# Down products of a gated MLP two blocks behind its gates, and the last down products of the MLP before it in one group

## The chip, the cores and the metric

The kernel runs on one core of a Trainium2 chip. The metric is the device time of one launch in microseconds. Before the change it is 898.23 us, the median of 3 runs (897.46 to 899.17).

## What is computed

Windowed attention (4 batches, 8 heads, 576 positions, head width 64), then a first MLP that takes the maximum of three products, then a gated MLP, on 2304 tokens of width 512, all in fp32:

```python
def _attn_ref(q, k, v):              # window 128, bias by head
    scores = np.where(mask, scale * q @ k.T + bias, -1e9)
    return softmax(scores) @ v
def _moe_ref(x, w1, w2, w3, w_out):  # 512 -> 768 -> 512
    h = np.maximum(np.maximum(x @ w1, x @ w2), x @ w3)
    return h @ w_out
def _moe2_ref(x, w_gate, w_val, w_out):  # 512 -> 1536 -> 512
    g = x @ w_gate
    silu = g * (1.0 / (1.0 + np.exp(-g)))
    return (silu * (x @ w_val)) @ w_out
```

## The kernel before

**Arithmetic.** TensorE multiplies in fp32r. Every fp32 operand is split into a head (rounded to fp32r) and a rest (value minus head), and a product of two operands is three matmuls: head by head, head by rest, rest by head. `mm3` (L111 to L113) does this for the up products of the first MLP and the gate and value products of the second; L547 to L549 do it for the down products of the second.

**Splitting the weights.** `prep_w` turns a raw weight piece of 128x512 into head and rest: one activation on ScalarE (L90, into `wf`), three operations on VectorE (L93, L94, L96), the cast of the head on ScalarE (L99), and the rest on VectorE (`low`, L77). It is done for 18 up pieces `w` of the first MLP (`prep_up`), its down pieces `wo`, and 36 pieces `u` of the second MLP (`prep`: gate, value and down piece of each of 12 blocks of the hidden width).

**Splitting the activations.** GpSimd rounds heads with `pool_round` (L80) and takes rests with `low` (L77): `x` from the attention, `h` from the first MLP, `a` from the gated product. In `gate`, ScalarE takes the sigmoid (L532), VectorE multiplies twice (L533, L534) into `sg`, and GpSimd makes head and rest of `a`.

**The stages.** The tokens of a batch fall into two sub-blocks of 256 and 320 tokens; there are eight, in the list `order`. For each the attention runs in steps (scores, normalise, transpose, values `pv`), `up_groups` gives 18 groups of 12 matmuls, and `down_groups` four rows of output in three groups, 72 matmuls in all. `spread` writes the groups of one list with the steps of others in between, so that attention steps and weight preparation stand among the products. The second MLP goes through five chunks of up to 512 tokens; a block (c, f) is 24 gate and value matmuls and 12 down matmuls for one twelfth of the hidden width. Before, `gate` of the next block stands ahead of the `down` of this one. `load_y` fetches the first MLP's output, which `down_groups` stores to `y_dram`; `YAT` is the block at which the next chunk's is loaded.

**What sets the order.** A scheduler orders each engine's instructions from the written order and priorities: `high_priority` pulls a piece forward; `keep_in_program_order`, used in `prep_w` where `pinned` is true, holds the first activation (L90) in its written place. Each engine then works through its own list in order.

**Buffers that matter here.** PSUM: four tiles of the pool `ps_m`, shared by the up and down groups and the gates; one tile `pv` for the attention's values; four tiles `ps_o` for the second MLP's output. The values of a unit leave `pv` by one ScalarE copy (L394) and three VectorE additions (L395, and L397 twice) into `xr`, and GpSimd splits `xr` into `x`.

Of the kernel before, what the change touches and what calls it, by code (L numbers as in the profile page):

```python
# [23 lines left out]
NF1, NF2 = F1 // P, F2 // P  # L24
# [5 lines left out]
CHUNKS = [(t, min(TB, NT - t)) for t in range(0, NT, TB)]  # L30
FILL = -float(2.0 ** 100)

RAWS = 4
C0, C1, C2, C3 = 5, 6, 12, 15
HIGH, EARLY = 100, 3
NORM = "aa"
A2, A3 = 4, 2
D6 = 0
WARM, WN = 24, 256
NORM0, K0 = "pp", 4  # L40
AH = 0, 100
A1, E1 = 3, 0
YAT = 8
LN, LT, LV = 1, 2, 4

LEAST = 1.0 * 2.0 ** -15
PIN = False


@with_exitstack  # L50
def kernel(ctx: ExitStack, tc, q0, k0, q1, k1, qk0, qk1, vv, w123, wo1, wgv, wo2, out):
# [87 lines left out]
    def up_groups(b, s):  # L139

        n = SUBS[s][1]
        m = {}

        def group(f, e):
            xt = x_t[b, s]
            ps = ps_m.tile([P, 512], F32, tag="m", name="ps1")
            for k in range(KD):
                mm3(ps[:, :n], w1[f, e], k * P, xt[k][:, 0, :n], xt[k][:, 1, :n], k == 0, k == KD - 1)
            with tc.high_priority(HIGH):
                if e == 0:  # L150
                    m[f] = tmp.tile([P, 320], F32, tag="m0", name="m0")
                    nc.scalar.copy(m[f][:, :n], ps[:, :n])
                else:
                    nc.vector.tensor_tensor(out=m[f][:, :n], in0=ps[:, :n], in1=m[f][:, :n], op=ALU.max)
                if e == 2:
                    ht = hp.tile([P, 2, n], F32R, tag=f"h{s}", name=f"h{s}", bufs=NF1)
                    pool_round(ht[:, 0, :], m[f][:, :n])
                    low(nc.gpsimd, ht[:, 1, :], m[f][:, :n], ht[:, 0, :])
                    hs[b, s, f] = ht

        return [lambda f=f, e=e: group(f, e) for f in range(NF1) for e in range(3)]

    def down_groups(b, s):
        t0, n = SUBS[s]
        t0 += b * S

        def part(ps, d, ks):
            for k in ks:
                ht = hs[b, s, k]
                mm3(ps[:, :n], wo[k], d * P, ht[:, 0, :], ht[:, 1, :], k == 0, k == NF1 - 1)  # L170

        def group(ds):

            ps = [ps_m.tile([P, 512], F32, tag="m", name="ps2") for d in ds]
            for i, d in enumerate(ds):
                part(ps[i], d, range(NF1 - 1))
            for i, d in enumerate(ds):
                part(ps[i], d, [NF1 - 1])
                with tc.high_priority(HIGH):
                    y = tmp.tile([P, 2, 320], F32R, tag="y", name="y")  # L180
                    nc.scalar.copy(y[:, 0, :n], ps[i][:, :n])
                    low(nc.vector, y[:, 1, :n], ps[i][:, :n], y[:, 0, :n])
                nc.sync.dma_start(
                    out=y_dram[:, d * P:(d + 1) * P, t0:t0 + n].rearrange("a p n -> p a n"),
                    in_=y[:, :, :n].bitcast(F32),
                )

        return [lambda ds=ds: group(ds) for ds in ((0, 1), (2,), (3,))]

    order = [(b, s) for b in range(B) for s in range(2)]  # L190
# [4 lines left out]
    prep = ea("prep", 4)  # L195
# [253 lines left out]
    for t in range(len(units) + LV):  # L449
# [9 lines left out]
        if t < len(units):  # L459
            u = units[t]  # L460
            if u.j == BLOCKS[u.s][0]:
                i = todo.index((u.b, u.s, u.p))
# [6 lines left out]
    def attn_units(i):  # L469
        return steps[done_at[i]:done_at[i + 1]]  # L470

    def spread(main, *others, early=0):


        done = [0] * len(others)
        for i, g in enumerate(main):
            for n, o in enumerate(others):
                while done[n] < len(o) and done[n] * (len(main) - early) <= i * len(o):
                    o[done[n]]()
                    done[n] += 1  # L480
            g()
        for n, o in enumerate(others):
            for piece in o[done[n]:]:
                piece()
# [90 lines left out]
    conv = [lambda f=f, e=e: prep_up(f, e) for f in range(NF1) for e in range(3)]  # L575
# [9 lines left out]
    spread(up_groups(*order[2]), a3[len(a3) * A3 // 8:], early=EARLY)  # L585
    for i in range(3, len(order) - 1):
        spread(down_groups(*order[i - 1]) + up_groups(*order[i]), attn_units(i + 1), early=EARLY)
    for g in down_groups(*order[-2])[:D6]:
        g()
    actx.close()  # L590
    raws2 = en("raws2", RAWS)
    w2pool = en("w2pool")
    ps_o = en("ps_o", 4, space=PSUM)
    prep, load_y, gate, down = second(w2pool, raws2, ps_o)
    conv = [lambda f=f, i=i: prep(f, i) for f in range(NF2) for i in range(3)]
    spread(down_groups(*order[-2])[D6:] + up_groups(*order[-1]), [lambda: load_y(0, [0])] + conv[:C2])
    spread(down_groups(*order[-1]), [lambda: load_y(0, [1])] + conv[C2:C3])

    spread([lambda: gate(0, 0)], conv[C3:C3 + 3])
    blocks = [(c, f) for c in range(len(CHUNKS)) for f in range(NF2)]
    for n, (c, f) in enumerate(blocks):
        if c == 0:
            for piece in conv[C3 + 3 + 3 * f:C3 + 6 + 3 * f]:
                piece()
        if f == YAT and c + 1 < len(CHUNKS):
            load_y(c + 1)
        if n + 1 < len(blocks):
            gate(*blocks[n + 1])  # L610
        for t in range(CHUNKS[c][1] // P):
            down(c, t, f)

# [55 lines left out]
```

## Time and profile before

| what | value |
|---|---|
| median of 3 runs | 898.23 us (897.46 to 899.17) |
| profiled execution | 900.01 us |
| its span | 898.3 us |
| mean granted clock of TensorE | 0.996 |
| TensorE matmul (PE) busy | 878.1 us, 98% |
| VectorE (DVE) busy | 464.6 us, 52% |
| GpSimd (POOL) busy | 409.3 us, 46% |
| ScalarE (ACT) busy | 349.5 us, 39% |

The profiled execution is a single one; its own time contains its span and 1.7 us around it. The shares are averages over the whole span. The attention and the first MLP take about the first half, and the other engines are busy mostly there: in the page's forty slices VectorE is at 0.6 to 0.9 up to the twenty-third and at 0.1 in nearly all of the rest. A stretch must therefore be read by itself. Granted clock 1.00 is 2.4 GHz for TensorE, 0.50 is 1.2 GHz. The end of a matmul in the trace is modelled, so that one row overlaps the next; the distance of two starts is the better measure of its cost.

### The profile page before, as it was taken

How to read it: one execution, taken by the hardware profiler on the slowest of the kernel's cores; microseconds unless marked ns; L12 is line 12 of the kernel's file. 1: busy time of each engine (PE TensorE's matmuls, PEld its weight loads, DVE VectorE, ACT ScalarE, POOL GpSimd, SP SyncE). 2: the span in 40 equal slices, each digit the busy share in tenths (PEclk: the TensorE clock that was granted, in tenths of full speed). 3: DMA queues.
4: the chain of work that ended last, by engine and by line, in shares of the span. 5: the costliest groups of instructions: out<-in, count | busy, mean ns of one | idle time of the engine just before them, and what ended most of it. 6: DMA issues, size and time to landing. Idle time of an engine off the chain costs nothing.

```text
span 898.3 us, 14855 instructions
## 1 busy us (share of the span) xinstructions
PE 878.1 (98%) x5280; PEld 778.7 (87%) x5280; DVE 464.6 (52%) x1293; ACT 349.5 (39%) x1004; POOL 409.3 (46%) x599
## 2 busy tenths in 40 slices
PE   8998999999999999999998999999999999999998
PEld 6677899999999999999886788888888888888897
DVE  7689956867687776848999811111111111111111
ACT  6789656856486656614554301000110001000101
POOL 5587666766777586554325421222122212221222
PEclk9899999999999999999999999999999999999999
DMA  9844414415232431325755504000210002000100
GB/s 324 281 122 128 135 45 153 126 55 148 67 113 60 137 99 51 116 93 170 257 184 176 165 0 141 1 1 1 93 48 1 1 21 73 1 1 1 47 1 24
DMA packets 40873, 82.22 MB, mean 92 GB/s; under 512 B 3680, under 2 KB 16992, under 8 KB 40800
## 3 DMA queue, kind: packets, MB, share of 16 engines
q1 hardware_dynamic: 39712, 79.18, 27.5%
q10 hardware_dynamic: 1088, 2.10, 0.7%
q8 instruction: 42, 0.69, 0.3%
q14 instruction: 31, 0.25, 0.1%
HBM read 67.11 MB, written 14.16 MB: 90 GB/s over the span
## 4 chain that ended last, share of the span: by engine, by line
PE 81%; issue 6%; POOL 5%; DVE 4%; DMA 1%; ACT 1%; ACTq 0%; SPq 0%; POOLq 0%; DVEq 0%
PE ps L111 10%; PE pg L111 10%; PE pg L112 10%; PE pg L113 10%; PE ps L113 10%; PE ps L112 10%; PE po L549 5%; PE po L547 5%; PE po L548 5%; PE pv L390 2%; PE pt L349 2%; POOL a L80 1%; PE sc L299 1%; PE sc L304 1%; PE sc L303 1%
## 5 line engine op out<-in xcount | busy, mean ns | idle before, releaser
L80 POOL TENSOR_SCALAR a<-sg 128x512 fp32r<-128x512 f32 (+1 forms) x60 | 44.5, 742 | 331.8 <-DVE sg L534 328.5
L113 PE MATMUL pg<-y,u 128*128 128x512 f32 (+1 forms) x480 | 176.6, 368 | 0.0
L112 PE MATMUL pg<-y,u 128*128 128x512 f32 (+1 forms) x480 | 176.5, 368 | 0.0
L111 PE MATMUL pg<-y,u 128*128 128x512 f32 (+1 forms) x480 | 176.5, 368 | 0.0
L113 PE MATMUL ps<-x,w 128*128 128x256 f32 (+1 forms) x576 | 173.5, 302 | 1.6 <-DVE w L77 1.5
L111 PE MATMUL ps<-x,w 128*128 128x256 f32 (+1 forms) x576 | 173.3, 304 | 1.2 <-ACT w L99 1.2
L112 PE MATMUL ps<-x,w 128*128 128x256 f32 (+1 forms) x576 | 172.3, 300 | 1.9 <-POOL x L77 1.9
L533 DVE TENSOR_TENSOR sg<-pg,sg 128x512 f32<-128x512 f32 (+1 forms) x60 | 38.2, 637 | 253.8 <-ACT sg L532 253.8
L532 ACT ACTIVATE sg<-pg 128x512 f32<-128x512 f32 (+1 forms) x60 | 33.2, 553 | 325.2 <-PE pg L113 321.8
L113 PEld LDWEIGHTS ps<-x,w 128*128 128x128 f32 x576 | 109.2, 190 | 4.2 <-DVE w L77 2.4
L111 PEld LDWEIGHTS ps<-x,w 128*128 128x128 f32 x576 | 109.0, 190 | 4.0 <-ACT w L99 1.5
L112 PEld LDWEIGHTS ps<-x,w 128*128 128x128 f32 x576 | 109.2, 190 | 2.7 <-POOL x L77 2.1
L111 PEld LDWEIGHTS pg<-y,u 128*128 128x128 f32 x480 | 90.5, 188 | 15.5
L112 PEld LDWEIGHTS pg<-y,u 128*128 128x128 f32 x480 | 90.5, 188 | 15.3
L113 PEld LDWEIGHTS pg<-y,u 128*128 128x128 f32 x480 | 90.5, 188 | 15.1
L365 POOL TENSOR_SCALAR_AFFINE_SELECT t<-pk 128x512 fp32r<-128x512 f32 (+3 forms) x128 | 72.7, 590 | 34.7 <-PE pv L390 14.5
L549 PE MATMUL po<-u,a 128*128 128x512 f32 x216 | 84.2, 392 | 2.8 <-POOL a L77 2.8
L547 PE MATMUL po<-u,a 128*128 128x512 f32 x216 | 84.4, 391 | 0.3 <-POOL a L80 0.3
L548 PE MATMUL po<-u,a 128*128 128x512 f32 x216 | 84.2, 390 | 0.0
L77 POOL TENSOR_TENSOR a<-sg,a 128x512 fp32r<-128x512 f32 (+1 forms) x60 | 72.4, 1206 | 5.0
L317 ACT ACTIVATE z<-z,mn 128x128 f32<-128x128 f32 (+1 forms) x160 | 63.3, 399 | 21.8 <-DVE mn L312 21.8
L534 DVE TENSOR_TENSOR sg<-pg,sg 128x512 f32<-128x512 f32 (+1 forms) x60 | 38.2, 637 | 60.3 <-PE pg L113 60.1
(91 smaller groups left out, 1672.4 us busy)
## 6 DMA issues: line engine op xcount, KB each, us to landing
wr<-wgv SPq DMA_DIRECT2D x24, 512.0 KB, 4.2
qkr<-qk SPq DMA_DIRECT2D x24, 416.0 KB, 3.4
wr<-w SPq DMA_DIRECT2D x18, 512.0 KB, 5.2
wr<-wo SPq DMA_DIRECT2D x12, 512.0 KB, 3.9
y<-y_dram SPq DMA_DIRECT2D x12, 512.0 KB, 4.1
y_dram<-y SPq DMA_DIRECT2D x16, 320.0 KB, 2.4
out<-ob SPq DMA_DIRECT2D x18, 256.0 KB, 2.1
y_dram<-y SPq DMA_DIRECT2D x16, 256.0 KB, 2.9
```

Source lines behind the costliest of these rows:

```text
L77: eng.tensor_tensor(out=out, in0=raw, in1=head.bitcast(F32), op=ALU.subtract)
L80: nc.gpsimd.tensor_scalar(out=out, in0=in_, scalar1=1.0, scalar2=1.0, op0=ALU.mult, op1=ALU.mult)
L111: nc.tensor.matmul(ps, wh, xt_h, start=first, stop=False)
L112: nc.tensor.matmul(ps, wh, xt_l, start=False, stop=False)
L113: nc.tensor.matmul(ps, wl, xt_h, start=False, stop=last)
L317: nc.scalar.activation(out=z[:m, a], in_=z[:m, a], func=AF.Exp, scale=-1.0, bias=mn[:m, a:a + 1], accum_out=sm[:m, a:a + 1],)
L365: nc.gpsimd.affine_select(out=t[:, i, :n, :, :m], in_=w[:, :n, :, :m], compare_op=op, fill=0.0, base=0, pattern=[[0, n], [0, 2], [-sign, m ...
L533: nc.vector.tensor_tensor(out=sg, in0=pair[0], in1=sg, op=ALU.mult)
L534: nc.vector.tensor_tensor(out=sg, in0=pair[1], in1=sg, op=ALU.mult)
L547: nc.tensor.matmul(po, ah, w2[f, 2][:, 0, :], start=f == 0, stop=False)
L548: nc.tensor.matmul(po, ah, w2[f, 2][:, 1, :], start=False, stop=False)
L549: nc.tensor.matmul(po, al, w2[f, 2][:, 0, :], start=False, stop=f == NF2 - 1)
```

## The change

It changes five things.

1. In the second MLP, the gates of two blocks stand ahead of the first `down`, and inside the loop `gate` runs two blocks ahead instead of one.
2. The pieces `u` are prepared in the order in which this needs them: gate and value pieces of two blocks, then for each block f the gate and value pieces of f + 2 and the down piece of f.
3. The down products of the last sub-block but one are no longer ahead of the last up products: they come behind them, in one list with the down products of the last sub-block. 18 pieces instead of 15 are written ahead of the first gates.
4. `PIN`: the first activation of each up piece keeps its written place on ScalarE. `C0`: four instead of five up pieces are prepared beside the first attention steps.
5. `YAT`: the next chunk's input is loaded at block 6 instead of 8.

```diff
-C0, C1, C2, C3 = 5, 6, 12, 15
+C0, C1, C2, C3 = 4, 6, 12, 18
...
-D6 = 0
...
-YAT = 8
+YAT = 6
...
-PIN = False
+PIN = True
...
-    for g in down_groups(*order[-2])[:D6]:
-        g()
...
-    conv = [lambda f=f, i=i: prep(f, i) for f in range(NF2) for i in range(3)]
-    spread(down_groups(*order[-2])[D6:] + up_groups(*order[-1]), [lambda: load_y(0, [0])] + conv[:C2])
-    spread(down_groups(*order[-1]), [lambda: load_y(0, [1])] + conv[C2:C3])
-    spread([lambda: gate(0, 0)], conv[C3:C3 + 3])
     blocks = [(c, f) for c in range(len(CHUNKS)) for f in range(NF2)]
+    need = [(f, i) for f in range(2) for i in range(2)]
+    for f in range(NF2):
+        need += [(f + 2, i) for i in range(2) if f + 2 < NF2] + [(f, 2)]
+    conv = [lambda f=f, i=i: prep(f, i) for f, i in need]
+    spread(up_groups(*order[-1]), [lambda: load_y(0, [0])] + conv[:C2])
+    spread(down_groups(*order[-2]) + down_groups(*order[-1]), [lambda: load_y(0, [1])] + conv[C2:C3])
+    spread([lambda: gate(0, 0), lambda: gate(0, 1)], conv[C3:C3 + 3])
     for n, (c, f) in enumerate(blocks):
...
-        if n + 1 < len(blocks):
-            gate(*blocks[n + 1])
+        if n + 2 < len(blocks):
+            gate(*blocks[n + 2])
         for t in range(CHUNKS[c][1] // P):
             down(c, t, f)
```

The lines of the helpers move up by one (L111 to L113 become L110 to L112), those of the second MLP too (L547 to L549 become L546 to L548).

What this does to the engines' lists is shown at three places. The first is TensorE's list at the end of the attention. Before, the last but one `pv` stands inside the third group of down products of the last sub-block but one (`ps` with `h` and `wo`):

```order
L111 MATMUL ps_6402<-h_6259,wo_1731 128x256
L112 MATMUL ps_6402<-h_6259,wo_1731 128x256
L390 MATMUL pv<-t,v 128x256 x4
L113 MATMUL ps_6402<-h_6259,wo_1731 128x256
L111 MATMUL ps_6402<-h_6331,wo_1819 128x256
L112 MATMUL ps_6402<-h_6331,wo_1819 128x256
L113 MATMUL ps_6402<-h_6331,wo_1819 128x256
```

and the last one (64 columns by two) inside the second up group of the last sub-block (`ps` with `x` and `w`), 34 matmuls later:

```order
L113 MATMUL ps_6458<-x_5637,w_0_0_236 128x320
L111 MATMUL ps_6483<-x_5637,w_0_1_305 128x320
L112 MATMUL ps_6483<-x_5637,w_0_1_305 128x320
L113 MATMUL ps_6483<-x_5637,w_0_1_305 128x320
L390 MATMUL pv<-t,v 128x2x64 x4
```

In the changed kernel both stand among the first four up groups of the last sub-block:

```order
L111 MATMUL ps_6395<-x_5637,w_0_2_398 128x320
L112 MATMUL ps_6395<-x_5637,w_0_2_398 128x320
L110 MATMUL ps_6422<-x_5637,w_1_0_483 128x320
L111 MATMUL ps_6422<-x_5637,w_1_0_483 128x320
L112 MATMUL ps_6422<-x_5637,w_1_0_483 128x320
L389 MATMUL pv<-t,v 128x256 x4
L389 MATMUL pv<-t,v 128x2x64 x4
L110 MATMUL ps_6356<-x_5637,w_0_0_236 128x320
L110 MATMUL ps_6371<-x_5637,w_0_1_324 128x320
L110 MATMUL ps_6395<-x_5637,w_0_2_398 128x320
L110 MATMUL ps_6422<-x_5637,w_1_0_483 128x320
```

The two `pv` now follow each other directly, and behind them come the fourth quarters of the four up groups, which read the part of `x` that the last `pv` gives.

The second place is TensorE's list at the first down product of the second MLP (`po` from `a` and a down piece `u`; `pg` is a gate or value product). Before, 55 matmuls of `pg` stand ahead of it:

```order
L112 MATMUL pg<-y,u_6646 128x512
L113 MATMUL pg<-y,u_6646 128x512
L111 MATMUL pg<-y,u_6646 128x512
L547 MATMUL po<-u_6497,a_7009 128x512
L548 MATMUL po<-u_6497,a_7009 128x512
```

In the changed kernel 72 do, six whole tiles:

```order
L110 MATMUL pg<-y,u_6544 128x512
L111 MATMUL pg<-y,u_6544 128x512
L112 MATMUL pg<-y,u_6544 128x512
L546 MATMUL po<-u_6569,a_7039 128x512
L547 MATMUL po<-u_6569,a_7039 128x512
L548 MATMUL po<-u_6569,a_7040 128x512
```

From there on a block of 24 `pg` and one of 12 `po` alternate in both, with the `po` one block further behind.

The third is ScalarE's list in the first steps (`z` are the exponentials of the attention, `x` and `xr` its values, `tn` and `pk` transposed pieces, `wf` and `w` the up pieces). Before:

```order
L99 CAST w_0_0_236<-wr 128x512
L90 ACTIVATE wf<-wr 128x512
L384 CAST x_328<-pv 128x128
L385 COPY xr<-pv 128x128
L361 COPY pk<-pt 128x256
L317 ACTIVATE z,sm<-z,mn 128x128 x4
```

In the changed kernel:

```order
L98 CAST w_0_0_236<-wr 128x512
L383 CAST x_320<-pv 128x128
L384 COPY xr<-pv 128x128
L360 COPY pk<-pt 128x256
L316 ACTIVATE z,sm<-z,mn 128x128 x4
L383 CAST x_320<-pv 128x128
L384 COPY xr<-pv 128x128
L356 COPY tn<-pt 128x256
L89 ACTIVATE wf<-wr 128x512
```

The activation into `wf` that followed the cast of the first piece now stands behind `x`, `xr`, `pk`, four exponentials, the next `x` and `xr`, and `tn`.

## Rows read from the trace of the kernel before

**Rows 1.** Busy time by stretch; columns as in its first line, sums left out.
```profile
core 0: us, PE busy (x) PEld busy (x) DVE busy (x) ACT busy (x) POOL busy (x), PEclk, DMA share, GB/s
24.00:27.00 3.00, 1.10 (x8) 0.90 (x8) 2.08 (x6) 1.86 (x7) 2.91 (x6) 1.00 1.05 381
27.64:34.47 6.83, 6.83 (x27) 4.98 (x27) 3.42 (x13) 3.31 (x13) 2.73 (x7) 0.50 1.05 384
60.00:93.00 33.00, 28.77 (x217) 23.27 (x216) 31.71 (x94) 29.33 (x102) 25.90 (x41) 1.00 0.47 147
400.00:434.00 34.00, 34.00 (x238) 34.00 (x237) 27.30 (x53) 15.85 (x29) 13.46 (x13) 1.00 0.54 172
434.00:437.00 3.00, 1.85 (x13) 1.59 (x11) 3.00 (x8) 1.25 (x2) 2.92 (x2) 1.00 0.66 204
437.00:455.00 18.00, 17.69 (x99) 16.15 (x100) 15.89 (x28) 11.11 (x19) 2.31 (x3) 1.00 0.90 302
455.00:505.00 50.00, 46.83 (x201) 37.08 (x200) 49.83 (x76) 22.35 (x38) 21.69 (x12) 1.00 0.51 160
505.00:894.00 389.00, 389.00 (x1850) 327.24 (x1848) 72.89 (x115) 39.78 (x72) 95.23 (x108) 1.00 0.09 30
```

**Rows 2.** Waits of TensorE: total us, times, longest us.
```profile
PE po L549 <- POOL a L77: 2.8, 4, 0.9
...
PE po L547 <- POOL a L80: 0.3, 1, 0.3
```

**Rows 3.** TensorE's timeline at 473 us: start, us, instruction, [idle before and releaser].
```profile
472.83 0.39 PE L112 MATMUL pg<-y,u 128*128 128x512 f32 x1
473.06 0.39 PE L113 MATMUL pg<-y,u 128*128 128x512 f32 x1
473.78 0.50 PE L547 MATMUL po<-u,a 128*128 128x512 f32 x1 [0.33 <-POOL a L80]
...
475.45 0.50 PE L549 MATMUL po<-u,a 128*128 128x512 f32 x1 [0.93 <-POOL a L77]
```

**Rows 4.** GpSimd's timeline at the same place.
```profile
473.81 1.58 POOL L77 TENSOR_TENSOR a<-sg,a 128x512 fp32r<-128x512 f32 x1
```

**Rows 5.** VectorE's timeline, first products of two gates in turn.
```profile
467.69 0.68 DVE L533 TENSOR_TENSOR sg<-pg,sg 128x512 f32<-128x512 f32 x1
...
476.80 0.68 DVE L533 TENSOR_TENSOR sg<-pg,sg 128x512 f32<-128x512 f32 x1
```

**Rows 6.** TensorE's timeline in the last down products of the first MLP.
```profile
435.40 0.31 PE L113 MATMUL ps<-h,wo 128*128 128x320 f32 x1
435.54 0.31 PE L111 MATMUL ps<-h,wo 128*128 128x320 f32 x1
437.31 0.41 PE L112 MATMUL ps<-h,wo 128*128 128x320 f32 x1 [1.46 <-POOL h L77]
```

**Rows 7.** Timeline of all engines, last two attention products `pv`.
```profile
398.55 0.64 PE L390 MATMUL pv<-t,v 128*128 128x256 f32 x4
...
399.03 0.27 PE L113 MATMUL ps<-h,wo 128*128 128x256 f32 x1
...
399.23 0.37 ACT L394 COPY c<-pv 64x256 f32<-64x256 f32 x1 [1.75 <-PE pv L390]
...
400.15 0.58 DVE L397 TENSOR_TENSOR xr<-pv,c 64x128 f32<-64x128 f32 x2
...
403.42 0.56 PE L390 MATMUL pv<-t,v 128*128 128x128 f32 x4
...
405.23 0.24 POOL L80 TENSOR_SCALAR x<-xr 128x64 fp32r<-128x64 f32 x1 [3.56 <-DVE xr L397]
...
405.91 2.35 ACT L99 CAST u<-wr 128x512 fp32r<-128x512 f32 x4 [1.64 <-POOL x L77]
...
408.46 0.43 ACT L152 COPY m<-ps 128x320 f32<-128x320 f32 x1 [0.21 <-PE ps L113]
```

**Rows 8.** Groups of VectorE from 12 to 93 us: count, busy us, mean ns.
```profile
L77 DVE TENSOR_TENSOR kl<-qkr,r 128x512 fp32r<-128x512 f32 x3 | 2.8, 946 | 0.0
```

**Rows 9.** Groups of ScalarE from 8 to 30 us, same columns.
```profile
L90 ACT ACTIVATE wf<-wr 128x512 f32<-128x512 f32 x5 | 3.4, 679 | 0.0
```

## Prediction, before the changed kernel had run

> **What bounds the kernel now.** I read the table by stretches of time first [rows 1]. From 505 us to 894 us TensorE is busy in every one of 389.00 us, so nothing moved there can shorten the time, only lengthen it. Room is left in four places alone: the first steps (24 to 34 us and 60 to 93 us), the turn of the last down products (434 to 437 us), and the stretch from 455 to 505 us, where VectorE is busy 49.83 of 50.00 us and TensorE only 46.83. The waits of TensorE [rows 2] then say for what: `a`, the rounded gate product from GpSimd, and `h`, the same for the first MLP. Its timeline at one such place [rows 3] shows the wait of L549 behind L77. Last I read who makes `a` late: GpSimd's L77, which ends at 473.81 + 1.58 = 475.39 us, just before the product that waits for it [rows 4], and ahead of it VectorE, whose products L533 of one block and of the next start 476.80 − 467.69 = 9.11 us apart [rows 5]. TensorE's 36 matmuls of a block take only 36 × 0.227 = 8.17 us (0.227 is the distance of two starts without a wait, 473.06 − 472.83, taken with one more digit over the run of them [rows 3]). The stretch is paced by weight preparation on VectorE.
>
> **Gates two blocks ahead: −3.9 us.** In each of four blocks the down products find their `a` not ready. The idle time is 2.8 + 0.3 = 3.1 us over five gaps [rows 2]. A matmul's row lasts 0.39 us though the next starts 0.227 us after it, so each gap is 0.16 us longer, measured from start to start, than the idle time: 3.1 + 5 × 0.16 = 3.9 us. With one more gate and one more down between an `a` and its use, 36 matmuls or 8.2 us are gained on a lateness that was 0.5 + 1.1 = 1.6 us in the worst block [rows 3], the two idle times there with 0.16 added to each. VectorE is not relieved by this, so what is late next has to be named: the four PSUM tiles of the gates, which L534 frees. Here the reordered preparations help: 21 of 36 stand ahead of or beside the first two gates instead of 18, and a value tile comes due only with its down. One preparation costs VectorE (9.11 − 2 × 0.68) / 3 = 2.6 us, 0.68 being an L533 [rows 5] or the L534 like it. Three moved forward are 7.9 us, and VectorE has 34.00 − 27.30 + 18.00 − 15.89 = 8.8 us free from 400 to 455 us [rows 1]. That fits, narrowly. Bounds: −3.9 if it does, 0 if the wait only changes its tile. I take −3.9, because the surplus of VectorE's work per block (0.94 us) over the five blocks left with preparations is 4.7 us, less than the 8.2 us gained.
>
> A rule speaks against it. The trace puts these repeating gaps down to GpSimd's L77 [rows 2, 3]. The Trainium skill's Perfetto Trace Analysis, section Optimization Strategy, says that the same gap repeating on the engine that should be saturated can mean too few SBUF or PSUM buffers for the next tile. By that rule, two gates ahead, which hold all four PSUM tiles, would bring nothing, and this term would be 0. The rows before show no TensorE wait for such a tile, and I go by them.
>
> **Last down products together: −1.6 us, and what they uncovered.** At 435.54 us one product starts and the next at 437.31 [rows 6]; less the normal step of 0.14 to 0.15 us that is 1.6 us, a wait for the last `h`. Afterwards the downs of the last sub-block but one stand between, 8.6 us of work (72 × 0.12 us, the step of 256 columns [rows 7]), against a lateness of 1.6: all of it goes. But those same downs stood beside the end of the attention, and now only the first up products do. Each use of the one PSUM tile of the attention product `pv` frees it late [rows 7]: started at 398.55, copied by L394 at 399.23, last read by the second L397 at 400.15 + 0.58 = 400.73 us. The order now puts the last `pv` right behind the last but one. That one takes 399.03 − 398.55 = 0.48 us of TensorE for its four matmuls, so the last waits 400.73 − 398.55 − 0.48 = **1.7 us**. The next products in the queue are the fourth quarters of the four open sums and need the head of the last `x`, which came 405.47 − 403.42 = 2.05 us after that `pv` started; it takes about half of 0.48 us itself, so TensorE waits another **1.8 us**. Queued behind are only products of the same sums, then a fifth sum that needs one of the four PSUM tiles back.
>
> That release comes from the ScalarE copy `m` (L152), and four casts `u` stand ahead of it: 2.35 us from 405.91, 0.44 us after the head of `x`, so the copy ends 0.44 + 2.35 + 0.43 = 3.2 us after that head. The twelve quarter products last 12 × 0.147 = 1.8 us (the step of 320 columns [rows 6]); the fifth sum would wait **1.4 us**.
>
> **TensorE's clock there.** The order makes a stretch of about 3.8 us in which TensorE has 0.7 us of work. The nearest rows [rows 1]: from 24 to 27 us it was busy 1.10 of 3.00 us, and from 27.64 us the granted clock was 0.50, that is 1.2 GHz, for 6.83 us; from 434 to 437 us it was busy 1.85 of 3.00 us, and 437 to 455 shows 1.00. Ours is emptier than the first, so I take it as slowed for the same time. That loses half of 6.83, 3.4 us. The twelve quarters then last 3.6 us and cover the copy `m`, so the 1.4 us go. Sum for this place: 3.5 + 3.4 = **+6.9 us** with the fall, 3.5 + 1.4 = +4.9 us without. Below, 0 would need other work in the queue, which the order excludes; above, 3.5 + 1.4 + 3.4 = 8.3.
>
> **First steps: −0.7 us.** The pinned L90 sends one activation of 0.68 us [rows 9] behind the copies `x`, `xr`, `pk` and four exponentials, so GpSimd's mask comes earlier; and one preparation fewer lies beside the first attention steps. Against that, the new order has three more `kl` on VectorE ahead of the last up weight tile, 3 × 0.946 = 2.8 us [rows 8], in a stretch (60 to 93 us) where VectorE is busy 31.71 of 33.00 us [rows 1]. If the early slow clock goes, up to 3.4 us come back. The bounds are −3.4 and +2.8; I take −0.7, nearest to the one operation whose move is certain.
>
> **What costs nothing.** The later loads of `y` are issued two blocks earlier on SP (`YAT` 6), in the full stretch, and only stores of results stand behind them. The stores of the moved downs leave SP some 40 us later; the load that reads them comes in that full stretch too, over 200 us on. The loads of the three weight pieces moved forward fall into 400 to 434 us, where the DMA share is 0.54 [rows 1]. Were that cover gone, a late piece would hold VectorE, not TensorE, by the time of one preparation, 2.6 us.
>
> **Sum.** −3.9 − 1.6 + 6.9 − 0.7 = +0.7 us, on 900.01 us of the profiled execution (span 898.3): 900.7. That execution is 1.8 us above the median of the runs, 898.23, so I forecast 898.23 + 0.7 = **898.9 us**.
>
> **Rivals.**
> A, the forecast: 898.9, its own range 896.2 to 901.6 (the first steps at −3.4 and +2.0). Chance 0.36.
> B, no fall of the clock at the attention's end. For it: 434 to 437 us passed with a gap of 1.6 us and no fall; against it, our stretch has two such gaps with 0.25 us between. −3.9 − 1.6 + 4.9 − 0.7 = −1.3: **896.9**. Chance 0.20.
> C, slower: the three `kl` ahead of the last up weight tiles delay the up products one for one, since VectorE has only 1.29 us free in 60 to 93 us. It decides once VectorE's added work passes those 1.3 us plus what the first steps gave; then −3.9 − 1.6 + 6.9 + 2.8 = +4.2: **902.4**. For it stands VectorE's share there; against it, that the operations displaced were only moved. Chance 0.25.
> D, the early slow clock is gone as well: −3.9 − 1.6 + 6.9 − 3.4 = −2.0, **896.2**, and with B 894.2. For it: the wait before it was a single one, for GpSimd. Against: GpSimd remains the slowest engine there. Chance 0.14.
> E, the change doesn't do what it says: two blocks ahead, the wait only moves to the gates' PSUM tiles. −1.6 + 6.9 − 0.7 = +4.6: **902.8**. The narrow fit of VectorE speaks for it; that the trace shows no such wait speaks against it. The Trainium skill's rule on repeating gaps (Perfetto Trace Analysis, Optimization Strategy) would have it so. Chance 0.05.
>
> **How the numbers follow.** 0.2% is 1.8 us, about what a measurement of this kernel can tell from none: under 896.4 is faster, over 900.0 slower. Faster: D's 0.14, half of B, 0.05 of A: 0.29. Slower: C, E and 0.05 of A: 0.35. The rest, 0.36, is the same. The range goes from 894.5 (nearly all of D) to 903.0 (C and E with little above). Cases of both signs hold much of the chance, so the likeliest one's range stands with A.
>
> **What would show it.** Right: no idle time of TensorE before L546 and L548 (the numbers of the down products after the change) and none for `h`; two waits of 1.7 and 1.8 us near 395 us, one for VectorE's last read of `pv`, one for GpSimd's `x`; then a granted clock of 0.50 for some 7 us. If the clock stays at 1.00 there, B holds. If the up products between 60 and 93 us run later than before, C holds. If gate products wait for L534, E. If the waits near 395 us are absent, the forecast is wrong at its largest term.

## The result: slower by 0.7%

The changed kernel takes 905.06 us (median, 904.34 to 905.90), the kernel before 897.85 us beside it; the ratio is 1.0074, with an interval of 1.0058 to 1.0090. The forecast was 898.9 us, the range 894.5 to 903.0. Its profiled execution took 905.29 us, of which 903.5 are the span, 5.2 us more than before. The medians differ by 7.2 us, 2.0 more, because the profiled execution of before (900.01 us) was itself 2.2 us above its median.

Two marks that stand in both traces split these 5.2 us. The first is the first down product of the first MLP (`ps` from `h` and `wo`); what lies ahead of it are the first steps. The second is the first gate product. Here they are in the kernel before, on TensorE's timeline (start, us, instruction):

```profile
132.70 0.28 PE L111 MATMUL ps<-h,wo 128*128 128x256 f32 x1
...
446.06 0.39 PE L111 MATMUL pg<-y,u 128*128 128x512 f32 x1
```

and in the changed kernel:

```profile
137.05 0.28 PE L110 MATMUL ps<-h,wo 128*128 128x256 f32 x1
...
456.35 0.39 PE L110 MATMUL pg<-y,u 128*128 128x512 f32 x1
```

The first steps end 137.05 − 132.70 = 4.35 us later. From there to the gates it takes 319.30 instead of 313.36 us, 5.9 more. From the gates to the end of the span it takes 447.15 instead of 452.24 us, 5.1 less. 4.35 + 5.9 − 5.1 = 5.2.

Busy times of the changed kernel in the stretches that matter (columns as in [rows 1]):

```profile
27.64:34.47 6.83, 6.83 (x48) 5.16 (x47) 5.40 (x23) 6.61 (x27) 4.29 (x11) 1.00 1.05 374
40.00:100.00 60.00, 49.84 (x362) 41.27 (x361) 57.10 (x169) 51.40 (x171) 40.90 (x65) 0.94 0.46 141
87.37:94.20 6.83, 6.05 (x28) 6.05 (x28) 6.83 (x19) 4.70 (x12) 2.82 (x3) 0.50 0.44 129
408.22:415.05 6.83, 6.20 (x24) 5.80 (x23) 4.69 (x9) 3.59 (x7) 1.32 (x2) 0.50 0.73 235
455.00:510.00 55.00, 55.00 (x248) 45.78 (x247) 53.11 (x86) 27.81 (x45) 23.67 (x11) 1.00 0.59 189
```

The stretch of the gates is full now, 55.00 us of 55.00, where [rows 1] had 46.83 of 50.00. The slow clock that [rows 1] shows from 27.64 us is gone in this execution, but there are two others, 6.83 us each: one at 87.37 us in the first steps, one at 408.22 us, at the attention's end. The waits of TensorE over the whole span (total us, times, longest) say what it waited for:

```profile
PE ps L112 <- DVE w L76: 6.0, 6, 2.4
PE pv L378 <- POOL t L364: 2.4, 1, 2.4
PE pv L389 <- DVE xr L396: 1.7, 1, 1.7
...
PE ps L110 <- POOL x L79: 1.6, 1, 1.6
...
PE ps L110 <- ACT m L151: 0.6, 1, 0.6
```

No row for `a` and none for `h` is left in this view. In their place stand 6.0 us for the rests of the up pieces `w` (VectorE) and 2.4 us for `t` (the transposed exponentials, masked by GpSimd, that the `pv` products read) in the first steps, and 1.7, 1.6 and 0.6 us at the attention's end.

### The profile page after: what moved, and what is told of

Its sections match the earlier page's. It is cut to its first block, busy times and chain, and to the rows that moved or that the text cites. A ratio compares the mean times of both kernels' runs of the same rounds, so it can differ in the third digit from the quotient of the medians.

```text
span 903.5 us, 14867 instructions
## 1 busy us (share of the span) xinstructions
PE 879.5 (97%) x5280; PEld 781.7 (87%) x5280; DVE 466.5 (52%) x1293; ACT 351.2 (39%) x1004; POOL 402.1 (45%) x599
## 3 DMA queue, kind: packets, MB, share of 16 engines
q1 hardware_dynamic: 39712, 79.18, 26.9%
## 4 chain that ended last, share of the span: by engine, by line
PE 89%; DVE 5%; ACT 2%; issue 1%; POOL 1%; DMA 0%; ACTq 0%; SPq 0%; DVEq 0%; POOLq 0%
PE pg L112 11%; PE pg L110 11%; PE pg L111 11%; PE ps L110 10%; PE ps L111 10%; PE ps L112 10%; PE po L546 5%; PE po L547 5%; PE po L548 5%; PE pv L389 2%; PE pt L348 2%; PE sc L298 1%; PE sc L303 1%; PE sc L302 1%; DVE wf L93 1%
## 5 line engine op out<-in xcount | busy, mean ns | idle before, releaser
L112 PE MATMUL ps<-x,w 128*128 128x320 f32 (+1 forms) x576 | 175.1, 305 | 6.0 <-DVE w L76 6.0
L110 PE MATMUL ps<-x,w 128*128 128x320 f32 (+1 forms) x576 | 173.8, 305 | 3.4 <-POOL x L79 1.6
L111 PE MATMUL pg<-y,u 128*128 128x512 f32 (+1 forms) x480 | 176.5, 368 | 0.0
L112 PE MATMUL pg<-y,u 128*128 128x512 f32 (+1 forms) x480 | 176.5, 368 | 0.0
L110 PE MATMUL pg<-y,u 128*128 128x512 f32 (+1 forms) x480 | 176.5, 368 | 0.0
L111 PE MATMUL ps<-x,w 128*128 128x320 f32 (+1 forms) x576 | 174.5, 303 | 1.5 <-POOL x L76 1.5
L112 PEld LDWEIGHTS ps<-x,w 128*128 128x128 f32 x576 | 111.0, 193 | 8.0 <-DVE w L76 7.3
L110 PEld LDWEIGHTS ps<-x,w 128*128 128x128 f32 x576 | 110.3, 193 | 7.0 <-POOL x L79 1.7
L111 PEld LDWEIGHTS ps<-x,w 128*128 128x128 f32 x576 | 111.2, 193 | 2.5 <-POOL x L76 1.8
L111 PEld LDWEIGHTS pg<-y,u 128*128 128x128 f32 x480 | 90.5, 188 | 15.5
L110 PEld LDWEIGHTS pg<-y,u 128*128 128x128 f32 x480 | 90.5, 188 | 15.4
L112 PEld LDWEIGHTS pg<-y,u 128*128 128x128 f32 x480 | 90.5, 188 | 15.0
L546 PE MATMUL po<-u,a 128*128 128x512 f32 x216 | 84.2, 390 | 0.0
L547 PE MATMUL po<-u,a 128*128 128x512 f32 x216 | 84.2, 390 | 0.0
L548 PE MATMUL po<-u,a 128*128 128x512 f32 x216 | 83.9, 389 | 0.0
L76 POOL TENSOR_TENSOR a<-sg,a 128x512 fp32r<-128x512 f32 (+1 forms) x60 | 74.4, 1240 | 5.0
```

What stands on the lines that cost most here:

```text
L76: eng.tensor_tensor(out=out, in0=raw, in1=head.bitcast(F32), op=ALU.subtract)
L110: nc.tensor.matmul(ps, wh, xt_h, start=first, stop=False)
L111: nc.tensor.matmul(ps, wh, xt_l, start=False, stop=False)
L112: nc.tensor.matmul(ps, wl, xt_h, start=False, stop=last)
L546: nc.tensor.matmul(po, ah, w2[f, 2][:, 0, :], start=f == 0, stop=False)
L547: nc.tensor.matmul(po, ah, w2[f, 2][:, 1, :], start=False, stop=False)
```

## The experiments

All ratios are to the kernel before, run on the same chip in the same series.

### The parts of the change

**First steps put back.** The two settings as before:

```diff
-C0, C1, C2, C3 = 4, 6, 12, 18
+C0, C1, C2, C3 = 5, 6, 12, 18
-PIN = True
+PIN = False
```

> The changed kernel with its two settings of the first steps put back (five up pieces beside the first attention steps, L89 not pinned). Its lists of instructions are those of the kernel before up to the last down products, so the first 392 us should be the same in both. Theory 1 (the first steps cost the changed kernel 4.3 us, the attention's end 6.0 us, the gates give back 5.1 us): 897.9 + 6.0 - 5.1 = 898.8 us. Rival (the later parts cost something by themselves that the traces hide): above 900.5 us.

900.55 us, ratio 1.0025 (1.0014 to 1.0036): most of the loss is gone. Theory 1 missed by 1.8 us, and the number is the rival's. The trace shows what the later parts cost by themselves: two waits of the last down products of the first MLP for `y`, VectorE's last read of the PSUM tile that they reuse. The changed kernel has no such wait:

```profile
PE ps L110 <- DVE y L76: 2.3, 2, 1.4
```

The first mark stands at 129.69 us against 137.05 in the changed kernel, on TensorE's timeline:

```profile
129.69 0.28 PE L110 MATMUL ps<-h,wo 128*128 128x256 f32 x1
```

and these are two early stretches in the table by time:

```profile
24.00:27.00 3.00, 1.10 (x9) 0.87 (x8) 2.03 (x6) 1.81 (x7) 2.91 (x6) 1.00 1.01 343
27.64:34.47 6.83, 6.83 (x46) 5.01 (x47) 5.49 (x22) 5.25 (x21) 3.89 (x8) 1.00 0.95 287
```

These rows hold a second thing. Up to the last down products this kernel has the lists of the kernel before, instruction for instruction, and the same 1.10 of 3.00 us busy from 24 to 27 us, yet its clock stays at 1.00 where [rows 1] has 0.50, and its first mark is 3.0 us earlier. The fall near 27 us in the profile of before was one of that execution, and not of every execution of these lists. Against like executions the first steps of the change thus lose 137.05 − 129.69 = 7.4 us, not 4.35.

**Pin taken away alone, four pieces kept** (only `PIN = False`).

> The changed kernel with L89 not pinned, four up pieces beside the first attention steps as in the change. Its VectorE list has two kl ahead of the last up piece, as before. Theory kl (the kl pulled ahead of the last up pieces delay them one for one): the first steps cost nothing, 898.8 us. Theory four pieces (the piece taken away from the first attention steps is missing for the rest of the first 95 us): the 4.3 us stay, 903.1 us.

899.71 us, ratio 1.0013 (1.0002 to 1.0023), first mark at 129.51 us. The four pieces cost nothing. Here too the last down products wait for `y`, 1.7 us in all. Theory four pieces falls; theory kl holds so far.

**Five pieces, pin kept** (only `C0 = 5`).

> The changed kernel with five up pieces beside the first attention steps, L89 pinned as in the change. Its VectorE list has four kl ahead of the last up piece (two before, five in the changed kernel). Theory kl: two thirds of 4.3 us stay, 901.7 us. Theory four pieces: 898.8 us.

906.79 us, ratio 1.0086 (1.0068 to 1.0104). The first mark is at 134.83 us, 5.1 later than without the pin. It is the pin that costs; both theories missed the number, and there is a new wait of a gate product, far from the pinned pieces, for VectorE's first multiplication of a gate, which frees a PSUM tile (the profile of this run):

```profile
PE pg L110 <- DVE sg L532: 1.7, 1, 1.7
```

From the gates to the end this execution takes 450.13 us, 2.9 more than the run with the first steps put back (447.20).

**The gates alone**, in the kernel before:

```diff
+    need = [(f, i) for f in range(2) for i in range(2)]
+    for f in range(NF2):
+        need += [(f + 2, i) for i in range(2) if f + 2 < NF2] + [(f, 2)]
...
-    spread([lambda: gate(0, 0)], conv[C3:C3 + 3])
+    spread([lambda: gate(0, 0), lambda: gate(0, 1)], conv[C3:C3 + 3])
...
-        if n + 1 < len(blocks):
-            gate(*blocks[n + 1])
+        if n + 2 < len(blocks):
+            gate(*blocks[n + 2])
```

> The kernel before with one part of the change alone: gates two blocks ahead and the pieces prepared in the order that needs them; down products, first steps and the load of y as before. Theory (the down products lose their waits and nothing else moves): 897.9 - 5.1 = 892.8 us, the wait of 1.6 us for h stays. Rival (VectorE still has 18 pieces to prepare beside the gates and only shifts the wait to the gates' PSUM tiles): 896 to 898 us, with waits of the gate products for the second multiplication L533.

893.32 us, ratio 0.9943 (0.9927 to 0.9960). This is the good part of the change by itself, and the only waits left from 395 to 890 us are these:

```profile
PE ps L110 <- POOL h L79: 0.8, 1, 0.8
PE pg L110 <- PE ps L112: 0.3, 1, 0.3
```

**The down products alone**, in the kernel before:

```diff
-    spread(down_groups(*order[-2])[D6:] + up_groups(*order[-1]), [lambda: load_y(0, [0])] + conv[:C2])
-    spread(down_groups(*order[-1]), [lambda: load_y(0, [1])] + conv[C2:C3])
+    spread(up_groups(*order[-1]), [lambda: load_y(0, [0])] + conv[:C2])
+    spread(down_groups(*order[-2]) + down_groups(*order[-1]), [lambda: load_y(0, [1])] + conv[C2:C3])
```

> The kernel before with one part of the change alone: the down products of the last sub-block but one moved behind the last up products; gates one block ahead, first steps as before. Theory (two waits at the attention's end, 1.8 and 1.8 us, then 6.8 us at the granted clock 0.50, less the 1.6 us of the wait for h): 898.5 + 6 to 7 = 904.5 to 905.5 us. Rival (the time lost there gives VectorE room to prepare pieces ahead, and the waits for a behind it shrink by as much): 901 to 902 us.

908.98 us, ratio 1.0107 (1.0090 to 1.0124), more than expected. With the gates one block ahead, the waits for `a` grew (2.8 and 0.3 us in [rows 2]):

```profile
PE po L547 <- POOL a L80: 2.6, 3, 1.8
PE po L549 <- POOL a L77: 2.6, 3, 0.9
PE ps L111 <- DVE y L77: 1.8, 2, 1.1
PE pv L390 <- DVE xr L397: 1.7, 1, 1.7
PE ps L111 <- POOL x L80: 1.5, 1, 1.5
```

The waits for `y`, 1.8 us, are here too. So the parts do not simply add: this one costs 10.1 us alone, but only some 7 beside the gates of the change (900.55 − 893.32 = 7.2), which hide what it does to `a`.

**Everything but the down products** (gates alone, with `C0 = 4` and `PIN = True`).

> The whole change but for the down products of the last sub-block but one, which stay ahead of the last up products (and 15 pieces ahead of the gates, load at block 8, as before): gates two blocks ahead, pinned, four pieces. Theory (the parts add up: gates alone 893.3 us, the pin 5.4 us as between the changed kernel and its run without the pin): 898.7 us, first steps as in the changed kernel. Rival (the parts do not add up, since the pin alters the lists of the later stages as well): over 901 us or under 896 us.

901.17 us, ratio 1.0043 (1.0027 to 1.0060). The pin costs 901.17 − 893.32 = 7.9 us here, near the 7.2 us of the first marks (137.34 against 130.11 us in the run of the gates alone), and more than the 5.4 us between the medians of the changed kernel and its run without the pin. The number lies in the rival's range, by 0.2 us; but its reason isn't seen, since the loss lies ahead of the first mark. The executions spread from 899.92 to 907.20 us, so that the median is a rough figure here.

### What in the pin costs

**Pinned for the first six pieces, and for the last twelve.** In the kernel before:

```diff
-        prep_w(raw, w1[f, e], pinned=PIN)
+        prep_w(raw, w1[f, e], pinned=f < 2)
...
+        prep_w(raw, w1[f, e], pinned=f >= 2)
```

> The kernel before with one part of the change alone, and that for a third of the pieces: L90 pinned for the first six up pieces, the other twelve free. Two kl stand ahead of the last up piece on VectorE, as before. Theory late pieces (the pin of the later pieces puts kl and other attention work ahead of the last up pieces, on a VectorE that is full from 60 to 93 us): no loss, 898.5 us. Rival early pieces (the pin of the first pieces leaves VectorE idle in the first 50 us and the whole chain is late from there): 902 to 904 us.

> The kernel before with L90 pinned for the last twelve up pieces and free for the first six. Four kl stand ahead of the last up piece on VectorE (two before). Theory late pieces: 902 to 904 us. Rival early pieces: 898.5 us. If both this and the run with the first six pinned lose about half, the loss is one of all pieces and neither theory holds alone.

903.95 us, ratio 1.0047 (1.0034 to 1.0061), and 911.10 us, ratio 1.0125 (1.0107 to 1.0143). Each part costs, one of them more than the whole. The first does so with two `kl` ahead of the last piece as before (first mark at 133.66 us against 129.7 without a pin): theory kl falls here, and of the two theories of this pair neither holds alone. Not all of either loss lies in the first steps: from the gates to the end the two take 2.7 and 1.7 us longer than the kernel before, with more waits for `a`, and the profile of the last twelve also has a fall of the clock at 26.9 us. What they wait for in the first steps differs too. The waits with the first six pinned:

```profile
PE sc L303 <- DVE rc L331: 2.5, 1, 2.5
PE sc L303 <- DVE mn L312: 2.0, 1, 2.0
```

with the last twelve:

```profile
PE ps L111 <- ACT w L99: 3.5, 2, 2.8
PE sc L303 <- DVE mn L312: 2.9, 1, 2.9
PE ps L113 <- DVE w L77: 2.2, 1, 2.2
```

and the stretches at the lower clock, first six pinned:

```profile
79.15:82.56 3.41, 3.23 (x15) 3.26 (x16) 3.05 (x12) 3.41 (x12) 0.67 (x1) 0.50 0.35 116
89.39:92.80 3.41, 3.41 (x18) 3.29 (x16) 3.41 (x11) 2.88 (x8) 1.56 (x2) 0.50 0.40 116
```

last twelve:

```profile
84.95:88.36 3.41, 3.41 (x18) 3.41 (x18) 3.41 (x10) 3.41 (x12) 1.85 (x3) 0.50 0.11 43
```

Once it is attention scores that wait for VectorE's softmax, once up products that wait for their piece. Common to both, and to the changed kernel, are waits of 2 us and more in one piece, and a fall of the clock beside one of them or more. Not beside each: the wait of 2.4 us for `t` near 57 us left the clock at 1.00 in the changed kernel, and a fall followed it in the run without the down products. In the runs without the pin that change nothing else in the first steps, the longest wait from 40 to 100 us is 1.4 us with five pieces and 1.0 us with four:

```profile
PE sc L298 <- DVE mn L311: 1.0, 1, 1.0
PE ps L112 <- DVE w L76: 1.0, 1, 1.0
```

and the clock is at 1.00 there, with VectorE as full as anywhere, 58.16 of 60.00 us against 57.10 in the changed kernel (table by time):

```profile
40.00:100.00 60.00, 55.56 (x409) 45.87 (x409) 58.16 (x171) 51.59 (x178) 40.34 (x69) 1.00 0.45 132
```

**Rests of the last six pieces on GpSimd**, in the changed kernel, and, not pinned, in the kernel with the gates alone:

```diff
-        prep_w(raw, w1[f, e], pinned=PIN)
+        prep_w(raw, w1[f, e], pinned=PIN, rest=nc.gpsimd if f >= 4 else nc.vector)
```

> The changed kernel, with the rests (L76) of the last six up pieces made on GpSimd instead of VectorE. Theory (in the pinned lists VectorE has too much left from 60 to 96 us, and TensorE's waits there come in lumps of over 2 us, after which the granted clock falls): six times 0.68 us leave VectorE, the waits shrink by 3 to 4 us and the fall of the clock near 87 us goes with them: 905.1 - 3.5 to - 7 = 898 to 901.5 us. Rival (the pinned L89 itself is late on ScalarE, and VectorE only waits for it): no change, 904 to 906 us.

> The kernel before with the gates two blocks ahead (the run of that part alone: 893.3 us), and the rests of the last six up pieces made on GpSimd instead of VectorE, not pinned. Theory (VectorE paces TensorE from 70 to 96 us here too): up to 4.1 us less, 889.5 to 892 us. Rival (there is no loss left that VectorE causes; GpSimd becomes late with the h): 893 to 896 us.

911.52 us, ratio 1.0145 (1.0128 to 1.0162), and 896.39 us, ratio 0.9974 (0.9961 to 0.9988), which is worse than the gates alone. Less work on VectorE made neither faster. The wait moved to GpSimd and grew:

```profile
PE ps L112 <- POOL w L76: 6.6, 3, 3.6
PE pv L378 <- POOL t L364: 2.4, 1, 2.4
```

This tells against VectorE's load as the cause, but not cleanly, since GpSimd was the later engine. The second of these runs shows that it need not be the pin: without it, one score product waits 2.5 us for `mn`, and the clock falls at 92.9 us. Neither theory of the first run had 911.52 us in its range.

**Seven pieces beside the first attention steps, pinned** (`C0, C1 = 7, 8`).

> The changed kernel, pinned, with seven up pieces beside the first attention steps instead of four (and eight instead of six by the next bound). Two kl stand ahead of the last up piece, as in the kernel before. Theory lateness (the pin keeps the pieces at their written places, so that VectorE does them too late; written earlier, they come in time): the 7 us that the first steps lost against the unpinned lists shrink by half or more, 898 to 901.5 us. Rival (with the pin the waits only change their place, as in the runs with a part of the pieces pinned): 904 to 908 us.

903.70 us, ratio 1.0072 (1.0050 to 1.0094), between the two theories. The first mark is at 133.90 us, 3.2 earlier than in the changed kernel, though this execution also had a fall of the clock at 26.7 us. That speaks for the lateness of the pieces as a part of the price, but one profile carries it: the ratio is that of the changed kernel (1.0074). A fall near 85 us came here too, after a wait of 1.9 us for `mn`, and the attention's end cost what it did before.

### The attention's end

**Two of the three groups put back ahead of the up products**, first steps as before:

```diff
+    downs = down_groups(*order[-2])
-    spread(up_groups(*order[-1]), [lambda: load_y(0, [0])] + conv[:C2])
-    spread(down_groups(*order[-2]) + down_groups(*order[-1]), [lambda: load_y(0, [1])] + conv[C2:C3])
+    spread(downs[:2] + up_groups(*order[-1]), [lambda: load_y(0, [0])] + conv[:C2])
+    spread(downs[2:] + down_groups(*order[-1]), [lambda: load_y(0, [1])] + conv[C2:C3])
```

> The changed kernel with the first steps of the kernel before, and with two of the three groups of the moved down products put back ahead of the last up products; the third stays behind them. Theory (54 down products at the attention's end cover the two waits nearly, so the clock does not fall, and 18 products are enough to cover the last h): the 1.6 us of the wait for h come on top of the gates' 5.2 us, 891.7 us, or up to 0.5 us more for what is left of the wait for x. Rival (the attention's end needs all three groups): a wait of over 1.5 us and a fall of the clock, 896 to 898 us.

895.79 us, ratio 0.9957 (0.9940 to 0.9974). From 390 us on TensorE waits 0.2 us for `x`, and not for `h`; but 1.2 us for the copy `m` behind the four casts `u`, so the gain over the gates alone is nothing. The profiled execution, 892.53 us, is near the theory's 891.7; the median is not, and the rival's wait and fall did not come.

**One group put back** (`downs[:1]`).

> As the run in which two of the three groups of the moved down products stay ahead of the last up products, but with the first group alone (36 products). The last but one and the last attention product then have 22 up products between them, 3.2 us against the 2.2 us that the PSUM tile takes, so the first of the two waits goes; the fourth quarters still stand right behind the last one, and their wait of 1.8 us stays. Theory (it takes both waits together to bring the clock down): granted clock 1.00, 893.3 + 1.8 - 1.6 + 1 for the copy m = 894.5 us. Rival (one wait of 1.8 us is enough): a stretch at 0.50 and 897 to 898 us.

897.88 us, ratio 0.9991 (0.9979 to 1.0003); 895.86 us in the profiled execution. The wait of 1.6 us for `x` stands there alone, and the clock stays. The waits from 390 us on:

```profile
PE ps L110 <- POOL x L79: 1.6, 1, 1.6
PE po L548 <- POOL a L76: 1.2, 1, 1.2
PE ps L110 <- ACT m L151: 1.2, 1, 1.2
```

and the stretch by time:

```profile
399.00:407.00 8.00, 5.26 (x36) 4.85 (x35) 4.11 (x9) 3.35 (x7) 1.20 (x4) 1.00 0.20 57
```

In this execution the one wait did not bring the clock down. Its time is 1.4 us above the expected one, for the 1.2 us of `a` and the copy. The median, though, is the rival's number. The other executions spread up to 901.8 us, and the slowest also has the lowest mean granted clock, 0.993 against 0.999 in the profiled one; where it fell there no trace shows. So that one wait is not enough is shown for one execution, not for the kernel; and the run with the first steps put back speaks against the theory, since its fall began at 397.77 us, where the first of its two waits was over and the second only beginning (timeline and table by time of that run):

```profile
397.16 0.63 PE L389 MATMUL pv<-t,v 128*128 128x128 f32 x4 [1.69 <-DVE xr L396]
399.34 0.90 PE L110 MATMUL ps<-x,w 128*128 128x320 f32 x2 [1.55 <-POOL x L79]
```

```profile
397.77:404.60 6.83, 5.28 (x20) 5.13 (x20) 4.11 (x9) 3.52 (x7) 1.25 (x5) 0.50 0.34 96
```

**The waits filled.** First steps as before, and 72 products that nobody reads:

```diff
+        last = u is units[-1]
+        if last:
+            fl = ps_t.tile([P, 2, P], F32, tag="pt", name="fl")
...
+            for n in range(72):
+                nc.tensor.matmul(fl[:, :, :m], v[:, u.kb, n % 2, :], u.t[:, n % 2, :, 1, :m], start=True, stop=True)
```

> The changed kernel with the first steps of the kernel before (the run of that: 900.5 us, two waits of 1.8 us at the attention's end, then 6.8 us at the granted clock 0.50), and 72 products of 128 columns into the idle transpose tile beside the last attention product: 11 ahead of the last but one, 34 between the two, 27 behind, some 0.07 us each; nobody reads them. They cost 0.8 us ahead and some 0.4 us more than the waits they fill. Theory (the emptiness of TensorE brings the clock down, and that is 3.4 us of the price of this place): granted clock 1.00 throughout and 900.5 - 3.4 + 1.2 = 898.3 us. Rival (the clock falls anyway, for what follows): 901.5 to 902 us.

904.16 us, ratio 1.0065 (1.0053 to 1.0077): slower, and neither expectation has that time, but the clock did not fall there. TensorE's timeline, and the stretch by time:

```profile
396.06 1.34 PE L400 MATMUL fl<-t,v 128*128 128x128 f32 x11
397.24 0.69 PE L395 MATMUL pv<-t,v 128*128 128x256 f32 x4
397.76 3.91 PE L400 MATMUL fl<-t,v 128*128 128x128 f32 x34
401.51 0.61 PE L395 MATMUL pv<-t,v 128*128 128x128 f32 x4
```

```profile
396.00:406.00 10.00, 10.00 (x89) 10.00 (x88) 1.72 (x7) 1.33 (x4) 1.32 (x4) 1.00 0.00 1
```

So far as one profile shows, the theory of the clock holds: with the emptiness filled there is no fall. The time missed in part because the filling was sized wrongly: 34 of these products take 401.51 − 397.76 = 3.75 us, 0.11 us each and not 0.07, so they fill a wait of 1.8 us with 3.75. Against the profile with the first steps put back this span is 4.9 us longer, and only 1.7 of these lie between the two marks; 1.1 lie in the first steps, where the clock fell at 26.7 us, and 2.1 behind the gates, where new waits for `a` and `sg` account for 1.1. Filling the emptiness with dead products costs more than it saves.

**Gates alone with four pieces** (`C0 = 4`, not pinned).

> The kernel before with the gates two blocks ahead and four instead of five up pieces beside the first attention steps, not pinned. The two runs without the pin stood 0.8 us apart in favour of four. Theory (four pieces alone cost nothing, and gain at most 0.8 us): 892.5 to 893.3 us. Rival (it was the chance of the early fall of the clock): up to 896 us.

894.64 us, ratio 0.9952 (0.9935 to 0.9969), in the rival's range and no difference from 893.32. Three of its executions take some 892 us at a mean granted clock of 0.999, the other five 894.6 to 896.9 us at 0.994 to 0.998. The gates alone are the best version found; both intervals lie below the kernel before and the changed one.

## Why the prediction was wrong, step by step

**Gates two blocks ahead, −3.9 us: right, and too small.** The five gaps are gone; the stretch from the gates to the end gained 5.1 us. The gaps that I added up are 4.0 of these. Another 0.8 are the product after each wait, whose successor comes 0.34 instead of 0.227 us later (0.335 us at 475.45), and a smaller gap at 510.9 us that I had not counted; 0.3 have no place. The rival that the wait would only move to the gates' PSUM tiles is refuted for the changed kernel: its trace has no such wait. It is real in other lists: the run with five pieces, pinned, shows one of 1.7 us, and three more runs one of 0.5 to 1.5 us. By the Trainium skill's rule on repeating gaps (Perfetto Trace Analysis, Optimization Strategy) buffers could have been short; here the trace's releaser, GpSimd's `a`, was the right reading.

**Last down products together, −1.6 us, and the two waits, +3.5 us: right for the changed kernel.** No wait for `h` is left. The timeline of TensorE in the changed kernel:

```profile
402.53 0.63 PE L389 MATMUL pv<-t,v 128*128 128x256 f32 x4
404.84 0.63 PE L389 MATMUL pv<-t,v 128*128 128x128 f32 x4 [1.68 <-DVE xr L396]
407.02 0.86 PE L110 MATMUL ps<-x,w 128*128 128x320 f32 x4 [1.55 <-POOL x L79]
...
410.26 0.64 PE L110 MATMUL ps<-x,w 128*128 128x320 f32 x1 [0.63 <-ACT m L151]
```

The last `pv` waits 1.68 us for VectorE's second read (1.7 forecast), the fourth quarters 1.55 us for the head of `x` (1.8 forecast). They came some 8 us later than I wrote, mostly for the first steps.

**The clock there, +3.4 us: right.** 0.50 for 6.83 us from 408.22. Of the wait for the copy `m`, which I had let go, 0.6 us stayed, since the fall began only 1.2 us after the first of the quarters that were to cover it. The stretch from mark to mark cost 5.9 us net; 6.9 − 1.6 = 5.3 was forecast. My reason was weaker than the outcome: the row that I took as the model, 1.10 of 3.00 us busy from 24 to 27 us and then a fall, has no fall behind it in the run with the first steps put back. And one term was left out. Without the pin the same move cost 6.8 to 8.1 us from mark to mark (320.17, 320.69 and 321.42 us instead of 313.36), of which 1.7 to 2.3 are the waits for `y`; in the changed kernel, later by then, they are absent.

**First steps, −0.7 us: this step failed.** I took the one activation "whose move is certain" as the price, and −3.4 to +2.8 as the bounds. The trace says +4.35 against the profile of before, and +7.4 against an execution with the same lists as before and no early fall of the clock. Three things were wrong in it. First, the pin moved far more than one activation: the four pieces cost nothing, the pin 5.1 to 7.5 us at the first mark (three pairs of runs; 5.4 to 7.9 us between their medians), and the lists of all engines differ from the first steps on. Second, the upper bound was the price of work moved (`kl`), while the loss came as waits and a clock: TensorE waits 6.0 + 2.4 us for `w` and `t`, against 1.0 and 1.5 us without the pin, none of these over 1.0 us, and the fall at 87.37 us takes half of 6.05 busy us, 3.0. Third, the fall of the clock at 27 us, which I counted as a loss that the change might give back, comes in some executions and not in others. That the gates gave back 1.2 us more than forecast was luck for the sum: without it the miss would be larger by as much.

**The rivals.** C named the side and the place; 902.4 was too little, and its mechanism, the `kl` pulled ahead, did not hold: the first six pinned lose 4 us at the first mark without it. B did not come, since the clock fell. D came in part: the early fall was absent, which is 3.0 us against the profile of before, but the later fall took its place.

**What stays open** is which shift in the lists makes the long waits. The pin is shown to be the cause, in whole and in parts. That pieces come late as a share of it is suggested by the run with seven, and by one profile only; with the first six pinned VectorE makes the last up piece's rest at 89.7 us, earlier than in the run with the first steps put back (92.0 us), and the first mark is still 4 us late. Why an unpinned list spreads its waits, none over 1.4 us but in the run with the rests on GpSimd, while the pinned ones gather them, was not isolated: the settings could be varied only through the scheduler, which reorders all engines at once. `YAT` and the 18 pieces ahead of the gates were not tried by themselves.

## What to carry to other kernels

When a change touches what a scheduler orders, compare whole lists, and bound the term by the waits and clock falls that a list of that stage can make, not by the length of the instruction that was pinned. Before work is moved away from a chain (here 72 products from beside the attention's last steps), count what remains in the in-order queue between each link: the two waits came out within 0.3 us of that count. And read a clock fall from more than one execution before pricing it.

## What the runs showed of the hardware

The same lists had the granted clock at 0.50 near 27 us in some executions and not in others, behind the same wait of 1.9 us for `x`: for 6.83 us in the profile of before, for 3.41 us in the run with filled waits, and not at all in the run with the first steps put back; the first mark stood at 132.70, 130.82 and 129.69 us. That alone is 3 us between executions of like lists. The 76 timed executions of the kernel before agree: the 46 with a mean granted clock of 0.999 or 1.000 have a median of 898.3 us, the 12 at 0.995 or 0.996 one of 900.3 us. At the attention's end two waits, of 1.7 and 1.6 us with 0.6 us of work between them, came with a fall in each of the seven profiles that had both, for 6.83 us in six and 3.41 us in one. In two of them it began when the second wait had not run yet. The one profile with a single wait of 1.6 us had none.

A product of 128 columns in two pieces of 64 took 0.11 us from start to start, hardly less than one of 256 columns (0.12 us). The attention scores of 128 columns in one piece took 0.06 us in the same traces; that the pieces make the difference was not tried by itself.
